# A new issue order on every engine, and a table of rooms for shared tiles, in a kernel of gated linear attention and top-2 expert attention

## The chip, the cores and the metric

One core of one Trainium2 chip runs the whole kernel in one launch. The metric is the device time of that launch in microseconds, as the median over runs; lower is better. The core's engines each run their own list of instructions in order: PE (TensorE, matrix products), DVE (VectorE), ACT (ScalarE, table functions and copies), POOL (GpSimd) and SP (SyncE, which here issues every DMA). They meet by semaphores.

## The reference

Two stages, for 4 batches, 8 heads, 768 time steps, head size 48; then 4 experts with heads of 64 over a model width of 384.

```python
# stage 1: gated linear attention with a complex decay, per head
a = (a_re, a_im) * min(|a|, 0.999) / (|a| + 1e-6)
for t in range(768):
    S = a[t] * S + k[t] v[t]^T          # complex state 48 x 48
    y[t] = q[t] . Re(S)
# stage 2: x = y with the heads side by side, [4, 768, 384]
w = softmax over the two largest of x @ w_gate
out = sum over experts e:  w_e * (causal softmax(q_e k_e^T / 8) v_e) @ wo_e
```

## The kernel before, in words

Stage 1 is done in chunks of 128 time steps. The running product of the decays becomes a sum of logarithms and a sum of angles, so that q and k can be turned by sines and cosines of the angle and scaled by exponentials; then a chunk is an ordinary masked product plus a term from the state of the chunk before.

`e_steps` makes this for one tile of 128 rows (three tiles, j = 0, 1, 2, per batch). Its steps, with the lines of the profile: squares and logarithms of the decay (L553, L558, and ACT's helper L360), inverses (L565, L569), the arctangent (L590), the angle in turns (L593), its running sum (L596), the wrap to one turn (L599 on POOL, L600 on DVE), the fold (L606), sine and cosine (L609, L610), the running sum of logarithms (L577), exponentials, and the products with q and k (L613, L616, L619, L625). Arctangent, sine and cosine need another function table than logarithm and exponential, so ACT visits that table: `visit` loads it (L370), runs the functions in it, and loads the first one back (L382). A load is an instruction of its own in ACT's list. Batch 0's three tiles share one visit at the start; the later tiles have one visit each, in which ACT also stands for them.

The results go through DMAs from SP into the layout of heads (`fm`, L664), and `p1_units` works on pairs of heads: transposes (`pk`, L686), scores of a chunk (`psc`, L693, masked on DVE into `pts`, L698), state updates (`pu`, L710, added on DVE into `wst1`, L720, copied by ACT to `tst`), and the output (`yu`, from `pts` at L731 and from the state `tst` at L738), which ACT copies to `x` and `yt`. `p2_units` is stage 2 on x: a split of x in two parts (`xth` on ACT, `xtl` on DVE, L777), values and gate (`pv`, L789), projections (`pp`, L838), a first pass for the row maxima (`pm`, L857 and L860), a regrouping by DMA (`stk`, L873 to L875), scores (`psS`, L908), the product with the values (`po`, L927), row sums (`dn`, L940), and the output projection (`pw`, L968).

Batch b's stage 2 lies beside batch b+1's stage 1. At the end of `attention_moe` every engine's instructions stand in a list in the order in which the program asked for them, and the table `ORDER` says in which order they are chained:

```python
for e, o in ORDER.items():
    for i, j in zip(o, o[1:]):
        tc.add_manual_dep(asked[e][j], asked[e][i].name, first_in, reason="order")
```

Two kinds of rooms matter. `ab` (decay and angles of a tile) and `qk` (q and k of a tile) have two rooms each, and batch 0's third tile lies in rooms that stage 2 uses later (`ab2`, `qk2`). PSUM's eight banks are two groups, three (`psa`: `pk`, `psc`, `pu`, `yu`) and five (`psu`: all else). A pool gives a new tile the next room by its own rule, and the tile waits until the room's last reader is done. `pace` and `hold` (L507 to L517) put idle products of a constant into PE's list, each waiting for a step of another engine.

Of the kernel before, what the change touches and what calls it, by code (L numbers as in the profile page):

```python
# [33 lines left out]
def pieces():  # L34

    out, f = [], 0
    while f < DM:
# [303 lines left out]
def attention_moe(ctx: ExitStack, tc: tile.TileContext, ak, vk, w, out):  # L341
# [882 lines left out]
    i, j = PL["lo"]  # L1224
# [72 lines left out]
```

## Time and profile before

| what | value |
|---|---|
| time, median of 3 runs | 543.96 us (542.48, 543.96, 556.38) |
| span of the profiled execution | 545.1 us |
| mean granted clock of TensorE | 0.921 |
| PE busy | 448.3 us (82% of the span) |
| ACT, DVE, POOL busy | 354.6, 349.4, 253.8 us |
| chain that ended last, by engine | PE 47%, DVE 17%, ACT 10%, DMA 10%, POOL 8%, issue 5% |

The span runs from the first instruction to the last. The profiled execution is a run of its own: its span is 1.14 us (0.2%) above the median of the runs. The granted clock is a share of 2.4 GHz; 0.5 is 1.2 GHz. The chain is followed back from the last instruction, at each step to what released it. In a timeline row the bracket says how long the engine stood idle ahead of the row and what ended that.

### The profile page before, as it was taken

Reading aid. Unit: us, or ns where it says so; the run is one execution under the profiler, and the core shown is the slowest. Engines: PE = TensorE matmul, PEld = TensorE weight load, DVE = VectorE, ACT = ScalarE, POOL = GpSimd, SP = SyncE. Lnnn points to the kernel's source line nnn. Section 1 sums busy time; section 2 is a strip of 40 time slices with the busy share of each in tenths; the row PEclk is TensorE's granted clock in tenths of the full one; section 3 lists DMA queues with packets and bytes.
Section 4 is the critical chain, followed back from the end, with each engine's and each line's share of the span. In section 5 each row is a group of like instructions: output and inputs, shape, how many; then the busy total and the mean of one; then the engine's idle time right before and its main releaser. Section 6 shows DMA issues by size and latency. Waiting matters only on the chain.

```text
span 545.1 us, 9176 instructions
## 1 busy us (share of the span) xinstructions
PE 448.3 (82%) x3376; PEld 348.7 (64%) x3376; DVE 349.4 (64%) x637; ACT 354.6 (65%) x751; POOL 253.8 (47%) x219
## 2 busy tenths in 40 slices
PE   0049996766895999986996998989599999989895
PEld 0016894665683775866784776669488876877564
DVE  6899845789548935667649472685883536456522
ACT  6827769948758557949469645887856547525363
POOL 5568614625255645825225482845423517202663
PEclk9988997789996998988695998999899999999989
DMA  8606492089331981499332675079542360456102
GB/s 334 273 0 174 118 298 74 13 194 220 98 88 30 259 191 37 125 226 212 111 84 58 203 162 152 8 169 242 133 117 59 80 133 16 134 127 140 35 2 87
DMA packets 23804, 71.10 MB, mean 130 GB/s; under 512 B 3312, under 2 KB 7632, under 8 KB 22736
## 3 DMA queue, kind: packets, MB, share of 16 engines
q1 hardware_dynamic: 23760, 70.53, 49.3%
q8 instruction: 26, 0.43, 0.3%
q14 instruction: 18, 0.15, 0.1%
HBM read 26.74 MB, written 4.72 MB: 58 GB/s over the span
## 4 chain that ended last, share of the span: by engine, by line
PE 47%; DVE 17%; ACT 10%; DMA 10%; POOL 8%; issue 5%; SPq 2%; ACTq 0%; POOLq 0%; DVEq 0%
PE po L927 6%; PE pp L838 6%; PE psc L693 5%; DMA stk<-qka 5%; POOL pe L931 4%; DMA ab<-in_ak_dram 4%; PE pm L857 3%; PE pw L968 3%; DVE ab L596 3%; PE psS L908 3%; PE pu L710 3%; ACT qk L360 3%; DVE qk L577 3%; PE psS L909 3%; PE dn L940 3%
## 5 line engine op out<-in xcount | busy, mean ns | idle before, releaser
L931 POOL TENSOR_TENSOR pe<-pe 128x512 f32<-128x512 f32 (+1 forms) x64 | 82.5, 1289 | 35.5 <-ACT r L360 15.8
L862 DVE TENSOR_REDUCE mx<-pm 128x1 f32<-128x384 f32 (+4 forms) x128 | 59.4, 499 | 25.1 <-PE pm L860 20.6
L360 ACT ACTIVATE pe<-psS 128x512 f32<-128x512 f32 (+2 forms) x96 | 47.1, 544 | 33.4 <-PE psS L909 30.7
L693 PE MATMUL psc<-fm 96*128 96x128 f32 x384 | 58.3, 292 | 8.4 <-ACT x L360 7.9
L915 POOL TENSOR_SCALAR_AFFINE_SELECT pe<-pe 128x256 f32<-128x256 f32 x48 | 24.6, 528 | 86.6 <-ACT pe L360 86.5
L360 ACT ACTIVATE qk<-qk 128x768 f32<-128x768 f32 (+5 forms) x105 | 56.3, 566 | 11.6 <-DVE qk L577 10.1
L693 PEld LDWEIGHTS psc<-fm 96*128 96x128 f32 x384 | 52.2, 204 | 10.4 <-ACT x L360 8.3
L908 PE MATMUL psS<-stk 128*128 128x256 f32 (+3 forms) x160 | 48.1, 335 | 3.9 <-DVE qka L845 1.4
L857 PE MATMUL pm<-qka,qz 128*128 128x384 f32 (+4 forms) x128 | 43.1, 404 | 5.1 <-POOL qk L581 3.1
L698 DVE TENSOR_TENSOR pts<-psc,keep 128x512 f32<-128x512 f32 x48 | 32.8, 684 | 20.3 <-PE psc L693 19.5
L509 PE MATMUL warm<-keep,identb 128*128 128x512 bf16 x44 | 15.7, 531 | 33.9 <-ACT ab L590 26.7
L909 PE MATMUL psS<-stk 65*128 65x256 f32 (+3 forms) x160 | 42.9, 309 | 0.8 <-DMA stk<-mr 0.8
L908 PEld LDWEIGHTS psS<-stk 128*128 128x128 f32 x160 | 31.3, 198 | 18.1 <-ACT xth L360 3.6
L738 PE MATMUL yu<-fm,tst 96*48 96x128 f32 x288 | 35.3, 288 | 8.3 <-ACT tst L360 8.3
L927 PE MATMUL po<-pe,v 128*64 128x256 f32 (+3 forms) x240 | 40.2, 423 | 0.3 <-POOL pe L915 0.3
L720 DVE TENSOR_TENSOR wst<-tst,pu 96x96 f32<-96x96 f32 x56 | 13.8, 246 | 38.8 <-ACT tst L360 17.2
L731 PE MATMUL yu<-pts,vt 128*64 128x128 f32 x360 | 38.5, 289 | 0.0
L360 ACT ACTIVATE tst<-wst,fm 96x48 f32<-96x48 f32 x112 | 31.0, 325 | 11.1 <-DVE wst L720 11.0
L710 PE MATMUL pu<-vt,kts 128*96 128x48 f32 x300 | 33.7, 248 | 3.1 <-DVE wst L720 3.1
L581 POOL TENSOR_TENSOR qk<-qk 128x768 f32<-128x768 f32 (+2 forms) x12 | 17.9, 1489 | 38.4 <-ACT qk L360 22.1
L710 PEld LDWEIGHTS pu<-vt,kts 128*96 128x96 f32 x300 | 30.7, 166 | 7.2 <-DVE wst L720 3.6
L565 POOL TENSOR_TENSOR ab<-ab 128x768 f32<-128x768 f32 x11 | 21.8, 1984 | 27.8 <-ACT ab L360 27.8
(143 smaller groups left out, 1184.2 us busy)
## 6 DMA issues: line engine op xcount, KB each, us to landing
fm<-qk SPq DMA_DIRECT2D x18, 578.2 KB, 6.0
ab<-in_ak_dram SPq DMA_DIRECT2D x12, 768.0 KB, 8.8
stk<-qka SPq DMA_DIRECT2D x16, 576.0 KB, 10.7
qk<-in_ak_dram SPq DMA_DIRECT2D x9, 768.0 KB, 5.7
stk<-qka SPq DMA_DIRECT2D x16, 384.0 KB
vt<-in_vk_dram SPq DMA_DIRECT2D x15, 384.0 KB, 7.2
fm<-qk SPq DMA_DIRECT2D x24, 192.8 KB, 3.7
out_dram<-ob SPq DMA_DIRECT2D x24, 192.0 KB, 1.9
```

Of the source, the lines that this page charges most:

```text
L360: ins = order["act"] = nc.scalar.activation(*a, **k)
L693: nc.tensor.matmul(p[:, cc, i, :], part(f, i, 1, c), part(f, i, 0, c), start=True, stop=True)
L698: nc.vector.tensor_mul(o, x, keep[:, None, :].to_broadcast([128, 4, C]))
L710: nc.tensor.matmul(pu[:, cc, i, :], kts[k][:, cc, i, :], v[c][:, i, :D], start=True, stop=True)
L731: nc.tensor.matmul(yu[64 * i:64 * i + 64, cc * C:(cc + 1) * C], v[2 * k + cc][:, i, :], pts[k][:, cc, i, :], start=True, stop=2 * k + cc == 0)
L738: nc.tensor.matmul(yu[64 * i:64 * i + D, cc * C:(cc + 1) * C], tst[c][:, i, :], part(f, i, 0, c), start=False, stop=True)
L857: nc.tensor.matmul(p[:, :s1 - s0], qz[:, e, tb * C:(tb + 1) * C], a[:, 3, s0:s1], start=True, stop=not last)
L862: nc.vector.reduce_max(m[:, col:col + 1], p[:, :s1 - s0], axis=AX.X)
L908: nc.tensor.matmul(y, s[:, 0, i * C:(i + 1) * C], s[:, 1, a0:t1], start=True, stop=False)
L909: nc.tensor.matmul(y, s[:65, 3, i * C:(i + 1) * C], s[:65, 2, a0:t1], start=False, stop=True)
L927: nc.tensor.matmul(po[64 * e:64 * e + 64, a0 - t0:t1 - t0], st.get("v2", v2)[:, i, pr, e], x[:, e], start=i == 0, stop=i == UNITS[g][-1][-1])
L931: on("sum").tensor_add(y, y, x)
```

## The change

Every list of `ORDER` is replaced. No instruction is added or removed, and each keeps its engine: PE 2480 matrix instructions, ACT 751, DVE 637, POOL 215 and SP 217 are the same set in both. Of PE's instructions 300 keep their place, and the others move by 12.9 places on average (67 at most); on ACT the mean is 4.9 (30), on DVE 4.2 (28), on SP 1.4, on POOL 1.0. Of 564 tiles in PSUM 305 follow another tile in their bank. The number of rooms of every tag stays. `pace(0)` no longer takes a tile.

```diff
 ORDER = {
-    'PE': (
-        0, 1, 2, 3, 4, 5, 6, 7, 8, 9, 10, 11, 12, 13, 14, 15, 16, 17, 18, 19, 20, 21, 22, 23, 24, 25, 26, 27, 28,
...
+    'PE': [
+        0, 1, 2, 3, 4, 5, 6, 7, 8, 9, 10, 11, 12, 13, 14, 15, 16, 17, 18, 19, 24, 25, 26, 27, 20, 21, 22, 23, 28, 29, 30, 31, 32, 36, 37, 38, 39, 40,
...
+SLOTS = {
+    'ab': [0, 1, 0, 1, 0, 1, 0, 1, 0, 1, 0, 1],
...
+    'psa': [0, 1, 2, 0, 1, 2, 0, 1, 2, 0, 1, 2, 0, 1, 2, 0, 2, 1, 2, 0, 1, 0, 1, 2, 0, 1, 2, 1, 0, 1, 2, 1, 1, 0, 2, 1, 0, 2, 2, 1, 1, 0, 2, 0, 0, 1, 2, 1, 0, 2,
...
+class Rooms:
+    def __init__(self, pool, bufs):
+        self.pool, self.bufs, self.made = pool, bufs, {}
+
+    def tile(self, shape, dtype, name, tag=None, bufs=None):
+        tag, bufs = tag or name, bufs or self.bufs
+        if tag in SLOTS:
+            i = self.made[tag] = self.made.get(tag, -1) + 1
+            tag, bufs = f"{tag}_{SLOTS[tag][i]}", 1
+        return self.pool.tile(shape, dtype, name=name, tag=tag, bufs=bufs)
...
-    sb = ctx.enter_context(tc.tile_pool(name="sb", bufs=2))
-    ps = ctx.enter_context(tc.tile_pool(name="ps", bufs=1, space=PS))
+    sb = Rooms(ctx.enter_context(tc.tile_pool(name="sb", bufs=2)), 2)
+    ps = Rooms(ctx.enter_context(tc.tile_pool(name="ps", bufs=1, space=PS)), 1)
...
     def pace(n):
-
+        if not n:
+            return
```

Line numbers of the changed kernel are lower by 7 up to `pace` and by 6 behind it, and its tile numbers by 3 or 4.

**First place: POOL in batch 0's start.** `ab_64`, `ab_66`, `ab2_68` are the angles of the three tiles, `qk_65`, `qk_67`, `qk2_69` their q and k. Before, POOL has:

```order
L593 TENSOR_SCALAR ab_66<-ab_66 128x768
L599 TENSOR_SCALAR ab_64<-ab_64 128x768
L599 TENSOR_SCALAR ab_66<-ab_66 128x768
L599 TENSOR_SCALAR ab2_68<-ab2_68 128x768
L616 TENSOR_TENSOR qk_65<-qk_65,ab_64 128x256 x2
L625 TENSOR_TENSOR qk_65<-qk_65,ab_64 128x256 x2
L616 TENSOR_TENSOR qk2_69<-qk2_69,ab2_68 128x256
L625 TENSOR_TENSOR qk_67<-qk_67,ab_66 128x256
```

With the change, where L593 is the wrap, L610 and L619 the products of k with sine and cosine, L575 and L581 the scaling of q and k:

```order
L593 TENSOR_SCALAR ab_64<-ab_64 128x768
L575 TENSOR_TENSOR qk_67<-qk_67 128x2x256
L593 TENSOR_SCALAR ab_66<-ab_66 128x768
L581 TENSOR_TENSOR qk2_69<-qk2_69 128x2x256
L619 TENSOR_TENSOR qk_67<-qk_67,ab_66 128x256
L610 TENSOR_TENSOR qk_65<-qk_65,ab_64 128x256
L593 TENSOR_SCALAR ab2_68<-ab2_68 128x768
L619 TENSOR_TENSOR qk_65<-qk_65,ab_64 128x256
L610 TENSOR_TENSOR qk_65<-qk_65,ab_64 128x256
L619 TENSOR_TENSOR qk_67<-qk_67,ab_66 128x256
L619 TENSOR_TENSOR qk_65<-qk_65,ab_64 128x256
```

The wrap of the third tile, `ab2_68`, moved from ahead of all products to behind two of them, which need sine and cosine of the first two tiles.

**Second place: SP at the end of batch 0's transfers.** `ab_516` and `qk_517` are the loads of batch 1's first tile (`ab_512` and `qk_513` with the change). Before:

```order
L664 DMA fm_258<-qk_65 64x1x514
L664 DMA fm_258<-qk_67 32x1x514
L664 DMA fm_258<-qk_67 96x1x514
L664 DMA fm2_266<-qk_67 96x1x514
L754 DMA x_322<-yt_411 16x3x256 x2
L664 DMA fm2_266<-qk_67 32x1x514
L664 DMA fm2_266<-qk2_69 64x1x514
L664 DMA fm3_509<-qk2_69 96x1x514 x2
L411 DMA ab_516<-in_ak_dram 128x1536
L416 DMA qk_517<-in_ak_dram 128x3x512
L411 DMA ab_520<-in_ak_dram 128x1536
```

With the change:

```order
L658 DMA fm_255<-qk_65 64x1x514
L658 DMA fm3_505<-qk2_69 96x1x514
L658 DMA fm2_263<-qk2_69 64x1x514
L404 DMA ab_512<-in_ak_dram 128x1536
L658 DMA fm3_505<-qk2_69 96x1x514
L409 DMA qk_513<-in_ak_dram 128x3x512
L404 DMA ab_516<-in_ak_dram 128x1536
L658 DMA fm2_263<-qk_67 96x1x514
L658 DMA fm2_263<-qk_67 32x1x514
L658 DMA fm_255<-qk_67 96x1x514
L658 DMA fm_255<-qk_67 32x1x514
L748 DMA x_319<-yt_408 16x3x256 x2
```

The load of batch 1's first tile moved ahead of five transfers to `fm` and of the pair to `x`, and that pair and four of the five now stand behind three loads.

**Third place: ACT at the last batch's first visit.** `kts_3712` and `tst_3687` (3708 and 3683 with the change) are copies for stage 1, `x_3671` (3667) the copy that empties the bank `yu_3664` (3660). Before, around the visit:

```order
L360 ACTIVATE ab_3404<-ab_3404 128x768 x2
L370 ACT_TABLE_LOAD
L609 ACTIVATE ab_2622<-ab_2622 128x768
L610 ACTIVATE ab_2622<-ab_2622,col_87 128x768
L590 ACTIVATE ab_3404<-ab_3404 128x768
L382 ACT_TABLE_LOAD
L360 ACTIVATE v2_103<-pv_3647 128x256
L360 ACTIVATE qk_3503<-qk_3503 128x3x256 x3
L360 ACTIVATE x_3671<-yu_3664 128x256
L360 ACTIVATE tst_3687<-wst1_3688,fm_3389 96x48 x2
L360 ACTIVATE v2_103<-pv_3697 128x256
L360 ACTIVATE kts_3712<-pk_3709 128x192
```

With the change:

```order
L353 ACTIVATE tst_3683<-wst1_3684,fm_3385 96x48 x2
L353 ACTIVATE kts_3708<-pk_3705 128x192
L353 ACTIVATE ab_3400<-ab_3400 128x768 x2
L363 ACT_TABLE_LOAD
L603 ACTIVATE ab_2618<-ab_2618 128x768
L353 ACTIVATE ob_3551<-pw_3544 128x384
L353 ACTIVATE ob_3625<-pw_3618 128x384
L353 ACTIVATE v2_103<-pv_3693 128x256
L604 ACTIVATE ab_2618<-ab_2618,col_87 128x768
L353 ACTIVATE tst_3688<-wst1_3689,fm_3385 96x48 x2
L353 ACTIVATE v2_103<-pv_3643 128x256
L353 ACTIVATE v2_103<-pv_3759 128x256
```

The copies `tst_3683` and `kts_3708` moved from behind the visit to ahead of it; `x_3667` stands four rows below the table load that ends the visit.

## Rows read from the trace of the kernel before

**Rows 1.** By stretch: length, engines' busy us, granted clock, DMA share, GB/s.
```profile
0.00:46.50 46.50, 12.63 (x32) 4.45 (x33) 39.63 (x56) 29.32 (x49) 28.62 (x28) 0.89 0.51 191
46.50:84.00 37.50, 37.39 (x397) 32.05 (x395) 25.62 (x52) 26.16 (x80) 19.10 (x16) 1.00 0.73 217
84.00:137.00 53.00, 35.31 (x206) 29.58 (x207) 41.80 (x61) 42.12 (x72) 25.38 (x18) 0.84 0.51 119
137.00:232.00 95.00, 84.28 (x663) 63.47 (x661) 58.65 (x107) 68.12 (x147) 50.55 (x42) 0.93 0.47 117
232.00:300.00 68.00, 55.38 (x376) 45.11 (x375) 47.91 (x91) 47.13 (x97) 24.84 (x17) 0.79 0.58 139
300.00:364.00 64.00, 60.43 (x468) 44.83 (x469) 37.03 (x62) 42.34 (x91) 36.28 (x32) 0.96 0.51 134
364.00:395.00 31.00, 23.88 (x181) 20.71 (x181) 23.05 (x42) 24.21 (x48) 14.53 (x9) 0.89 0.80 192
395.00:545.10 150.10, 138.97 (x1061) 108.49 (x1059) 75.70 (x171) 75.21 (x175) 54.48 (x59) 0.99 0.34 85
```

**Rows 2.** What TensorE waited for, whole run: total us, times, longest.
```profile
PE yu L738 <- ACT tst L360: 8.3, 5, 4.7
...
PE psc L693 <- ACT x L360: 7.9, 2, 4.9
```

**Rows 3.** POOL's timeline from 20 us: start, us, line, operation, tiles.
```profile
32.64 3.69 POOL L599 TENSOR_SCALAR ab<-ab 128x768 f32<-128x768 f32 x2 [1.69 <-DVE ab L596]
...
41.13 1.68 POOL L625 TENSOR_TENSOR qk<-qk,ab 128x256 f32<-128x256 f32 x2
...
59.08 6.05 POOL L625 TENSOR_TENSOR qk<-qk,ab 128x256 f32<-128x256 f32 x2 [0.86 <-DVE qk L616]
```

**Rows 4.** ACT's timeline from 36 us.
```profile
41.64 0.83 ACT L609 ACTIVATE ab<-ab 128x768 f32<-128x768 f32 x1
...
43.31 1.28 ACT L382 ACT_TABLE_LOAD   x1
```

**Rows 5.** DVE's timeline from 36 us.
```profile
35.56 2.44 DVE L600 SCALAR_TENSOR_TENSOR ab<-ab 128x768 f32<-128x768 f32 x2
...
39.38 1.29 DVE L613 TENSOR_TENSOR qk<-qk,ab 128x256 f32<-128x256 f32 x2
...
45.95 0.41 DVE L613 TENSOR_TENSOR qk<-qk,ab 128x256 f32<-128x256 f32 x1
...
60.27 1.75 DVE L501 TENSOR_TENSOR wlo<-wst,whi 128x1542 fp32r<-128x1542 f32 x1
```

**Rows 6.** PE's timeline from 46 us.
```profile
46.51 0.25 PE L686 MATMUL pk<-ident,fm 96*128 96x96 f32 x1
```

**Rows 7.** SP's queue from 36 us.
```profile
42.06 25.12 SPq L664 DMA_DIRECT2D fm<-qk  x26
...
71.32 0.59 SPq L411 DMA_DIRECT2D ab<-in_ak_dram  x1
```

**Rows 8.** The chain of waits, 60 to 137 us: start, us, what.
```profile
71.32 3.94 DMA ab<-in_ak_dram
...
77.12 1.47 POOL qk L553
```

**Rows 9.** ACT's timeline, 76 to 104 us.
```profile
82.67 1.28 ACT L370 ACT_TABLE_LOAD   x1
...
89.60 0.55 ACT L360 ACTIVATE tst<-wst,fm 96x48 f32<-96x48 f32 x2
```

**Rows 10.** ACT's timeline, 373 to 396 us.
```profile
376.81 1.28 ACT L370 ACT_TABLE_LOAD   x1
...
384.60 0.36 ACT L360 ACTIVATE x<-yu 128x256 f32<-128x256 f32 x1
```

**Rows 11.** PE's timeline, 382 to 396 us.
```profile
385.02 1.16 PE L693 MATMUL psc<-fm 96*128 96x128 f32 x8 [2.97 <-ACT x L360]
```

More of the change, by code (lines that the diff above doesn't have):

```diff
@@ L112 @@
 ORDER = {
[130 rows of a table removed]
-    ),
-    'Activation': (
[35 rows of a table removed]
-    ),
-    'DVE': (
[30 rows of a table removed]
-    ),
-    'Pool': (
[10 rows of a table removed]
-    ),
[11 rows of a table removed]
-    ),
-}
[101 rows of a table added]
+    'DVE': [
[22 rows of a table added]
+    'Activation': [
[27 rows of a table added]
+    'Pool': [
[15 rows of a table added]
+}
+SLOTS = {
[5 rows of a table added]
+    'psu': [0, 1, 2, 3, 4, 0, 1, 3, 4, 2, 0, 1, 3, 4, 2, 1, 0, 4, 3, 1, 3, 2, 0, 1, 0, 3, 4, 2, 1, 0, 3, 2, 4, 1, 3, 0, 2, 1, 3, 4, 2, 1, 4, 0, 2, 4, 3, 4, 1, 2,
[11 rows of a table added]
+    'psa': [0, 1, 2, 0, 1, 2, 0, 1, 2, 0, 1, 2, 0, 1, 2, 0, 2, 1, 2, 0, 1, 0, 1, 2, 0, 1, 2, 1, 0, 1, 2, 1, 1, 0, 2, 1, 0, 2, 2, 1, 1, 0, 2, 0, 0, 1, 2, 1, 0, 2,
[3 rows of a table added]
+    'kts': [0, 1, 0, 1, 0, 1, 0, 1, 0, 1, 0, 1, 0, 1, 0, 1, 0, 1, 0, 1, 0, 1, 0, 1, 0, 1, 0, 1, 0, 1, 0, 1, 0, 1, 0, 1, 0, 1, 0, 1, 0, 1, 0, 1, 0, 1, 0, 1, 0, 1],
+    'pts': [0, 1, 0, 1, 0, 1, 0, 1, 0, 1, 0, 1, 0, 1, 0, 1, 0, 1, 0, 1, 0, 1, 0, 1, 0, 1, 0, 1, 0, 1, 0, 1, 0, 1, 1, 0, 1, 0, 1, 0, 1, 0, 1, 0, 1, 0, 1, 0, 1, 0],
+    'tst': [0, 1, 2, 3, 4, 0, 1, 2, 3, 4, 0, 1, 2, 3, 4, 1, 0, 2, 3, 4, 1, 0, 2, 3, 4, 1, 0, 2, 3, 4, 1, 0, 2, 3, 4, 1, 0, 2, 3, 4, 1, 0, 2, 3, 4, 1, 0, 2, 3, 4,
[8 rows of a table added]
+}
+class Rooms:
[7 more added lines that the diff above has]
+        return self.pool.tile(shape, dtype, name=name, tag=tag, bufs=bufs)
 @with_exitstack
```

403 rows, old and new, of tables (ORDER, SLOTS) are left out of this document.

## The prediction

> **What bounds the kernel now.** I read the table by stretches first, then TensorE's list of waits, then the chain of waits and the engines' timelines at the places that the first two name. In the table [rows 1] a stretch's length less PE's busy time is PE's idle time. It is 33.9 us in 0 to 46.5, where stage 1 of batch 0 makes its first tiles; 0.1 up to 84; 17.7 in 84 to 137; 10.7 in 137 to 232; 12.6 in 232 to 300; 3.6 in 300 to 364; 7.1 in 364 to 395; and 11.1 behind that. So TensorE bounds most of the run, and an order can win only where it stands idle or at the lower clock. The granted clock is below 0.9 in three stretches behind the start: 0.84 in 84 to 137, 0.79 in 232 to 300 and 0.89 in 364 to 395 [rows 1]. The list of waits says what ends the idle time: output products that wait for a state copy of ACT, 8.3 us in five waits, 4.7 the longest, and chunk scores that wait for ACT's copy to x, which empties their bank, 7.9 us in two waits, 4.9 the longest [rows 2]. Both come from visits to the other function table. In the first, ACT loads the table at 82.67 and gets to the state copies at 89.60 [rows 9]. In the last batch it loads at 376.81 and gets to the copy to x at 384.60, and PE goes on at 385.02 after 2.97 us [rows 10, 11].
>
> **Part 1, batch 0's start: +4 us.** The wrap of the third tile now stands on POOL behind two products that need sine and cosine. Before, the second and third tile's wraps ended at 36.33 (32.64 + 3.69), ahead of all products, and the third sine began at 41.64 [rows 3, 4]. Now the DVE's list puts that tile's second wrap and fold behind ten products of the first two tiles. Ten products ran from 39.38 to 46.36 before, 7.0 us, some of them for the third tile (the first and the last stand in [rows 5]). The first sine comes some 1.3 us sooner, since a wrap and a fold no longer stand ahead of it; so the ten run from about 38.1 to 45.1. A wrap takes 1.22 (half of 2.44) and a fold 0.46 (a third of the time from 38.00 to the first product) [rows 5], so both end near 46.8 and the third sine is 5 us late. The table goes back 1.67 behind it, near 48.5 instead of 43.31 [rows 4]. On POOL the wrap, 1.85 us by half of the 3.69 for two, ahead of the cosine product and two products of 0.84 (half of 1.68) put the first product that the transfers wait for at an end near 45.6 instead of 42.0 [rows 3]. SP began its transfers at 42.06 [rows 7], PE its first pair at 46.51 [rows 6]; both move by 3.6, I take 4. Bounds: +2 if POOL's products run beside fewer DVE products than before, +6 if the third tile's 5 us come through whole. Nothing hides it: PE is busy 37.39 of the 37.5 us behind [rows 1], though idle products of a constant lie among them.
>
> **Part 2, batch 1's first tile: -9 us of waits, -2 of clock, +2 for ACT.** The load was issued at 71.32, landed after 3.94 us, and POOL began at 77.12, when the second load was there [rows 8]. It now passes seven transfers, at about 0.6 us of issue each (0.59 for the load itself, [rows 7]) 4.2 us; some 2 of the start's delay come back through products that it still stands behind. So it goes out near 68 to 69. More than that, its squares, logarithms and arctangent stand 25 places further ahead on ACT, between the copies of batch 0, and the first projections of batch 0's stage 2 stand on PE ahead of its last output products. The 4.7 us wait [rows 2] is covered by those. I estimate the tile's exponentials at 5 to 8 us sooner, and of the 17.7 us idle [rows 1] I take half, 9, as gone; bounds 3 (only the longest wait, less what follows late) and 14. The clock: 0.84 granted is 32% of the stretch at 1.2 GHz and the rest at 2.4 [rows 1]. Of the 35.31 us busy that is 11, which would take 5.6 less at the upper level. PE still waits at places, so I take 2; bounds 0 and 5.6. Against it stands ACT's own wait: a square of the new tile now lies in front of batch 0's state copies and waits for the load. If the load lands near 72 and ACT gets there near 70, PE's output products stand too. I take +2; bounds 0 and 5.
>
> At this place a row bears on the price. The two cosine products that POOL began at 59.08 took 6.05 us, against 1.68 for two at 41.13, and DVE's weight split of 1.75 us ran beside them [rows 3, 5]. In the new order the load stands behind the first of them, as the first of many transfers did before, so I add nothing.
>
> The Trainium skill, page "SBUF — State Buffer", section "Who interferes with whom", says that a DVE instruction with two inputs in SBUF contends with a GpSimd instruction that reads SBUF, and that the loser is fully blocked. The trace agrees: 6.05 against 1.68 us [rows 3]. By that rule, if both splits take the ports ahead of that product, the load would go out 3.5 us later (two splits of 1.75) and the forecast would be 535 us instead of 532.
>
> **Part 3, the later visits: -4 and -4 us.** In the last batch the state copies stand ahead of the visit, and the chunk scores take a bank emptied by such a copy, not by the copy to x. So the 2.97 us [rows 11] go, and with them part of the wait of the next state products, which stood behind them: 4 of the stretch's 7.1 us idle; bounds 0 and 6. At the visit whose wait is the 4.9 us the bank is changed in the same way, and the copy to x stands ahead: of the 4.9 us [rows 2] I take 3, and 1 for the clock, 0.79 there [rows 1]; bounds 0 and 7. What follows the copies there on ACT is the visit itself, which gets later by the copies (0.55 us for two, [rows 9]), so the sines of the next tile are late next; that is hidden by the tile's distance from its use.
>
> **Part 4, all else: -1 and +2 us.** In 137 to 232 the places move little: 1 of 10.7 us; bounds -4 and +2. In the stretches with little idle time (0.1, 3.6 and most of 11.1, [rows 1]) a new order finds nothing to win and can only lay waits: 305 new neighbours in PSUM, lists shaped to other durations. I take +2; bounds -4 and +6. Copies and products keep their durations, since nothing is added.
>
> **Sum.** +4 -9 -2 +2 -4 -4 -1 +2 = -12 us. The profiled span of 545.1 becomes 533.1. The span lies 1.14 above the median of the runs, so the forecast is 543.96 - 12 = 532.0 us.
>
> **The rivals.** (a) All gains come: ACT does not wait for the load, nothing new comes, and the waits in 137 to 300 shrink further. Then -9 -2 -4 -4 -1 is -20, and 4 more of the idle time in 137 to 300 pay for the start: 524 us. For it speaks that each named wait has its cause moved; against it, that the idle time behind each is a chain through ACT, DVE and POOL, and ACT is busy 42.12 of 53 us in 84 to 137 [rows 1].
>
> (b) The waits move instead of going: PE gets to the next thing that isn't there. Only the waits behind visits go (3 of 4.7, 3 of 4.9 and 2.97), less the start's 4 and 1 new: -4, 540 us. For it speaks DVE's and ACT's 41.80 and 42.12 us in 84 to 137 [rows 1], against it the 11 us in which they stand idle.
>
> (c) Slower: transfers to fm queued behind three loads. Four of the five now stand behind them. The first load took 3.94 us to land and the second 1.86 more (77.12 - 75.26) [rows 8]; three need 3.94 + 2 x 1.86 = 7.7 us. From 68 that is 76, and PE wants these tiles near 78. If the load goes out only at 72, as it does when the third tile's 5 us come through whole, the tiles land past 80, PE and ACT stand 4 us each in a stretch where PE was always busy, and the chain to 137 starts no sooner than before: +6 +4 +4, nothing of part 2, -6 of part 3: +8, 552 us. It decides from a load later than 71.32.
>
> (d) The order does not bind, because releases come in another order than the lists; then nothing moves, 544 us. Every list is chained whole, so I give this nothing of its own and count it with (b).
>
> **How the numbers follow.** The forecast has 0.44, (a) 0.20, (b) 0.22, (c) 0.14. 2% of the median, 10.9 us, is about what a measurement of this kernel can tell from no change: faster is below 533.1, slower above 554.8. Of the forecast's own range, 524 to 539, 0.27 lies on the faster side and 0.17 within; (a) is faster; (b) within; of (c) 0.06 is within and 0.08 beyond, by its bounds (+6 to +16). That makes 0.47 faster, 0.45 same, 0.08 slower. The range goes to 519, for (a) with the whole clock, and to 550, into (c).
>
> **What would show it.** Right: PE's first pair near 50, the table back near 48, the load of batch 1's first tile before 70, PE's idle time from 84 to 137 below 10 us, no wait over 2 us of chunk scores for a copy to x, and PE's idle time behind 395 unchanged. Wrong: a load after 71.3; PE waits for fm before 90; ACT standing over 4 us on the load; new waits above 3 us in 137 to 232 or 300 to 364; the clock in 84 to 137 not above 0.84.

## The result, and the profile after

The changed kernel takes 501.09 us (median of 4 runs, 495.03 to 504.97), against 545.91 for the kernel before beside it. The ratio is 0.912, with an interval of 0.904 to 0.920: 8.8% faster. That ratio compares the shorter runs of both kernels (of the changed one 497.82 and 495.03 us, at mean clocks of 0.966 and 0.976), while the profiled run is its longest, 504.97 us at 0.943, so the tables below are of a long run, and no profile shows where the shorter ones win 7 to 10 us more. The forecast was 532.0 us, and its range ended at 519, so the prediction was wrong: the sign is right, but the gain is over three times the size. The profiled execution has a span of 503.3 us, 41.8 less than before's 545.1.

The table by stretches of the changed kernel, cut where TensorE has done as many products as in [rows 1]; columns as there.

```profile
0.00:47.70 47.70, 12.42 (x32) 3.87 (x32) 40.16 (x58) 26.34 (x42) 29.11 (x28) 0.92 0.53 190
47.70:99.40 51.70, 50.02 (x397) 42.09 (x397) 34.01 (x61) 37.73 (x101) 21.63 (x21) 0.75 0.56 157
99.40:131.20 31.80, 28.29 (x209) 24.52 (x208) 25.76 (x47) 26.58 (x54) 15.70 (x11) 0.89 0.63 149
131.20:220.20 89.00, 82.37 (x666) 64.39 (x664) 68.12 (x110) 70.67 (x150) 52.92 (x45) 1.00 0.59 145
220.20:276.70 56.50, 50.38 (x378) 41.75 (x374) 44.00 (x88) 42.65 (x90) 23.75 (x17) 0.91 0.71 167
276.70:333.80 57.10, 55.89 (x470) 45.02 (x470) 39.29 (x65) 42.49 (x95) 36.66 (x33) 1.00 0.53 138
333.80:360.40 26.60, 22.62 (x185) 20.21 (x181) 19.66 (x47) 20.74 (x43) 9.72 (x6) 0.94 0.97 229
360.40:503.30 142.90, 135.15 (x1061) 109.21 (x1058) 77.86 (x170) 79.34 (x183) 58.50 (x62) 0.99 0.37 90
```

Row against row with [rows 1], in us of length: +1.2 in the start, +14.2 in the next stretch, -21.2, -6.0, -11.5, -6.9, -4.4 and -7.2; together -41.8. Up to 137 us of before that is -5.8, and behind it -36.0. Split another way: TensorE's idle time (length less its busy time) fell by 30.7 and its busy time by 11.1. Behind 137 the busy time fell by 16.5 for about as many products (2749 and 2760). The clock can account for the sum: one minus the clock, times the busy time of each row, is 24 us for the five rows of before and 7 for those of after. Over the whole run, where the products are the same, the same reckoning gives 35.4 and 24.9 us (0.921 of 448.3 us, 0.943 of 437.1), 10.5 of the 11.1. Row by row it fits less well (the last one lost 3.8 us of busy time at 0.99 in both, and what took them is open), since an equal number of products isn't the same products.

The waits of TensorE in the changed kernel, to set beside [rows 2]: total us, times, longest.

```profile
PE psc L687 <- ACT kts L353: 3.6, 1, 3.6
PE warm L503 <- ACT ab L603: 3.6, 1, 3.6
PE pk L680 <- DMA fm<-qk: 2.5, 4, 1.5
...
PE pk L511 <- DVE qk L613: 2.1, 4, 1.0
...
PE yu L732 <- ACT tst L353: 1.0, 3, 0.4
```

Both waits that the prediction was built on are gone: 8.3 us for state copies is 1.0, and 7.9 for the copies to x isn't in the list. Two stands of 3.6 us are new. One is in the start, for the third tile's late sine (the first row below); the other is at 346.20 in the last batch, where the scores now wait for another copy.

```profile
46.21 1.47 PE L503 MATMUL warm<-keep,identb 128*128 128x512 bf16 x4 [3.57 <-ACT ab L603]
```

A row that the prediction never read went with them: the idle products of `hold`, which wait for VectorE's product of q with the cosine, 2.1 us here. In the waits of before that row was:

```profile
PE pk L517 <- DVE qk L619: 8.4, 2, 5.2
```

### The profile page after: what moved, and what is told of

It reads as the page before. It is cut to its first block, busy times and chain, and to the rows that moved or that the text cites. A ratio compares the mean times of both kernels' runs of the same rounds, so it can differ in the third digit from the quotient of the medians.

```text
span 503.3 us, 9149 instructions
## 1 busy us (share of the span) xinstructions
PE 437.1 (87%) x3376; PEld 351.1 (70%) x3376; DVE 348.9 (69%) x637; ACT 346.5 (69%) x751; POOL 248.0 (49%) x219
## 5 line engine op out<-in xcount | busy, mean ns | idle before, releaser
L856 DVE TENSOR_REDUCE mx<-pm 128x1 f32<-128x384 f32 (+4 forms) x128 | 60.3, 499 | 12.5 <-PE pm L854 7.2
L687 PE MATMUL psc<-fm 96*128 96x128 f32 x384 | 63.6, 302 | 4.6 <-ACT kts L353 3.6
L909 POOL TENSOR_SCALAR_AFFINE_SELECT pe<-pe 128x256 f32<-128x256 f32 x48 | 22.9, 481 | 83.8 <-ACT pe L353 81.6
L687 PEld LDWEIGHTS psc<-fm 96*128 96x128 f32 x384 | 55.9, 210 | 9.0 <-ACT kts L353 4.5
L575 POOL TENSOR_TENSOR qk<-qk 128x768 f32<-128x768 f32 (+2 forms) x12 | 20.3, 1699 | 39.9 <-ACT qk L353 33.5
L704 PE MATMUL pu<-vt,kts 128*96 128x48 f32 x300 | 36.7, 257 | 0.6 <-DVE wst L714 0.6
L921 PE MATMUL po<-pe,v 128*64 128x256 f32 (+3 forms) x240 | 36.9, 396 | 0.0
L704 PEld LDWEIGHTS pu<-vt,kts 128*96 128x96 f32 x300 | 33.5, 176 | 4.8 <-issue 1.6
L503 PEld LDWEIGHTS <-identb 128*128 128x128 bf16 x44 | 5.3, 129 | 44.9 <-ACT ab L584 25.5
L353 ACT ACTIVATE kts<-pk 128x384 f32<-128x384 f32 (+1 forms) x48 | 20.4, 431 | 21.8 <-PE pk L680 15.4
L902 PEld LDWEIGHTS psS<-stk 128*128 128x128 f32 x160 | 29.6, 191 | 7.0 <-issue 3.4
```

The costliest lines, as they stand in the source:

```text
L353: ins = order["act"] = nc.scalar.activation(*a, **k)
L687: nc.tensor.matmul(p[:, cc, i, :], part(f, i, 1, c), part(f, i, 0, c), start=True, stop=True)
L704: nc.tensor.matmul(pu[:, cc, i, :], kts[k][:, cc, i, :], v[c][:, i, :D], start=True, stop=True)
L856: nc.vector.reduce_max(m[:, col:col + 1], p[:, :s1 - s0], axis=AX.X)
L902: nc.tensor.matmul(y, s[:, 0, i * C:(i + 1) * C], s[:, 1, a0:t1], start=True, stop=False)
L909: nc.gpsimd.affine_select(x[:, :, :C], x[:, :, :C], pattern=[[0, 2], [1, C]], base=0, channel_multiplier=-1, compare_op=OP.is_ge, fill=0.0)
```

## The experiments

All kernels compute the whole output. Most take the lists and rooms of one kernel up to a time in that kernel's profile, and those of the other behind. Their lines are shifted: L176 is ACT's copies, L334 `hold`, L436 the cosine product with q, L481 the transfers to fm, L510 `psc`, L548 and L555 `yu`, L186 and L198 the table loads.

### Where the gain lies: old and new order in halves

First the changed kernel again, with no edit, to see how far its runs differ.

> The changed kernel once more, on the same chip as the next three. Theory 1 (the granted clock of the stretch behind the start, 0.75 in the profiled run of 505 us, is what its slower runs lose): the time is 495 to 505 us; a profile of about 496 us shows PE busy some 8 us less than 437 with the difference between 48 and 99 us, and the same idle time, 66 us. Theory 2 (the slower runs lose by waits on other engines): PE idle time moves with the time, and the clock of that stretch does not.

Measured: 505.12 us (496.9 to 506.29, 4 runs), where before took 545.31 beside it. The profile is of a run of 504.75 us and shows a clock of 0.75 from 48.0 to 98.9 again; no run near 496 us was profiled, so the two theories can't be told apart. The runs of the changed kernel differ by some 2%, and a single profile of it isn't good to better than that.

```diff
 ORDER, SLOTS:
-    the changed lists and rooms
+    PE 32, ACT 48, DVE 56, POOL 24, SP 22 leading places of before (what begins before 46.4 us), the changed ones behind
```

> Order and rooms of before for all that began before 46.4 us (batch 0's start, up to PE's first pair), the new order and rooms behind it. Theory 1 (the third tile's late wrap costs at the start, PE stands 3.6 us on its sine, falls to 1.2 GHz and stays there): the stretch up to PE's 430th product, 99.4 us in the changed kernel's profile, ends 9 to 15 us sooner, and the whole takes 485 to 492 us. Theory 2 (the early part of the new order is a whole, and batch 1's early load needs its start): no gain or a loss, 496 to 508 us.

Measured: 501.81 us, ratio 0.9235 (0.918 to 0.929). The old start wins nothing. TensorE began as in before, but then stood 2.26 us for a transfer to fm, up to 55.15. The clock was 0.57 behind that, 0.50 from 60 to 68, and 1.00 again from 72.

```diff
+    PE 436, ACT 198, DVE 168, POOL 56, SP 72 leading places of before (up to 137 us), the changed ones behind
```

> Order and rooms of before for all that began before 137 us, the new ones behind. Theory 1 (each stretch keeps what the new order gains in it: 36 us lie behind 137 us by the two profiles, -5.8 us of offset there and -41.4 at the end): 506 to 514 us. Theory 2 (the later stretches gain because the front delivers sooner; the order behind 137 us is worth only the visits, 8 us and the clock): 525 to 538 us.

Measured: 508.52 us, ratio 0.936 (0.931 to 0.941). With the old order up to 137 us, and so with its 4.71 us wait for a state copy and its lower clock there, 36.8 us are won, where the changed kernel won 40.2 beside it (by the ratios 0.064, where the whole change has 0.088). So most of the gain lies behind 137, and is there without the new front. Its table behind that point, cut by the same counts:

```profile
136.60:162.00 25.40, 24.50 (x207) 19.07 (x207) 19.24 (x44) 20.67 (x49) 12.80 (x11) 1.00 0.31 88
162.00:221.80 59.80, 55.88 (x456) 44.07 (x458) 41.83 (x61) 45.60 (x98) 36.28 (x32) 1.00 0.59 154
221.80:276.30 54.50, 49.60 (x377) 41.56 (x372) 44.34 (x88) 42.58 (x90) 23.62 (x17) 0.91 0.72 172
276.30:334.30 58.00, 56.32 (x472) 45.17 (x470) 40.73 (x65) 42.76 (x95) 36.91 (x33) 1.00 0.53 136
334.30:362.40 28.10, 22.90 (x184) 20.53 (x181) 18.98 (x47) 20.80 (x43) 9.72 (x6) 0.88 0.90 217
362.40:505.30 142.90, 135.18 (x1061) 109.31 (x1058) 77.91 (x170) 79.46 (x183) 58.61 (x62) 1.00 0.37 90
```

Behind 220 each row is within 2.0 us of the changed kernel's, and the first two make 85.2, against 89.0 there and 95.0 in [rows 1].

```diff
+    PE 426, ACT 195, DVE 164, POOL 54, SP 69 leading places of the changed kernel (up to 131.2 us), before's behind
```

> The new order and rooms for all that began before 131.2 us in the changed kernel's profile, the old ones behind. Theory 1 (gains stay in their stretch): 5.8 us faster than before in a run like the profiled one and up to 14 in a run with the full clock behind the start, 530 to 540 us. Theory 2 (the front carries the gain through the run): 505 to 520 us.

Measured: 548.1 us (539.88 to 551.52), where before took 545.31: no gain that four runs with this spread can show. Its table shows where the front's 6 us went. It is at 130.80 where before is at 137.2, and has lost them by the end of the next row:

```profile
0.00:130.80 130.80, 88.87 (x634) 69.59 (x636) 99.75 (x164) 90.51 (x195) 66.42 (x58) 0.86 0.58 168
130.80:170.50 39.70, 29.22 (x211) 22.77 (x207) 25.77 (x51) 27.60 (x55) 18.41 (x16) 0.89 0.39 94
```

Rows of ACT and TensorE say where:

```profile
139.37 1.36 ACT L176 ACTIVATE qka<-pp 128x512 fp32r<-128x512 f32 x3 [3.64 <-DMA stk<-qka]
...
141.23 1.89 PE L334 MATMUL psS<-keep,identb 128*128 128x512 bf16 x4 [2.52 <-DVE mr L699]
...
170.49 0.50 PE L334 MATMUL pk<-keep,identb 128*128 128x384 bf16 x1 [5.21 <-DVE qk L436]
```

In before, the second of these stands here, with no wait ahead of it:

```profile
141.43 1.04 PE L517 MATMUL psS<-keep,identb 128*128 128x512 bf16 x4
```

So the lead is gone at 141. TensorE waits there for `mr`, a small step of VectorE (which is busy 10.22 of the 10.43 us up to then), and ACT's copy waits for the regrouping transfers. The last of these went out at 126.54, in before at 126.40, though TensorE was 6 us further, and it kept ACT until 139.37, in before until 135.53. By 149 x4 is 0.4 us behind before, and from 151 on 1.3 us, down to the product at 170.49, which in before began at 169.18 after 5.20 us. A front that brings TensorE forward doesn't bring these transfers forward with it.

### The clock in the start

```diff
- 'n3': (8, 8, 0, 0, 8, 2, 2, 4, 0),
+ 'n3': (8, 8, 0, 0, 8, 2, 14, 4, 0),
```

This adds twelve idle products behind the second tile's cosine, into the 3.57 us for which TensorE stood for the third tile's sine.

> The changed kernel with 12 more idle products in PE's list, behind the second tile's cosine, where PE then stood 3.6 us for the third tile's sine. Theory 1 (PE falls to 1.2 GHz because it stands there, and the stream of small products behind does not bring the clock back for 25 us): the clock between 48 and 72 us is near 1 instead of 0.50, PE's busy time in the stretch up to its 428th product falls from 49.4 by 8 to 12 us, and the whole takes 490 to 497 us in every run. Theory 2 (that stretch waits on the tiles of stage 1, and a faster PE only stands more): PE's idle time there grows by what its busy time loses, 500 to 506 us.

Measured: 504.15 us (494.04, 502.17, 506.14, 507.62), ratio 0.9253 (0.915 to 0.936). The profile is of the 494.04. First the changed kernel's clock from 46 us on (columns of [rows 1]; the clock is the third number from the end):

```profile
46.00:50.00 4.00, 3.66 (x13) 2.22 (x13) 3.37 (x6) 3.97 (x9) 3.08 (x5) 0.58 0.81 180
50.00:54.00 4.00, 3.92 (x22) 3.96 (x23) 2.97 (x6) 2.56 (x9) 2.85 (x3) 0.50 0.86 207
...
66.00:70.00 4.00, 4.00 (x28) 3.35 (x28) 3.88 (x5) 1.58 (x7) 1.88 (x1) 0.50 0.71 136
70.00:74.00 4.00, 4.00 (x19) 1.73 (x16) 0.25 (x1) 1.88 (x8) 0.70 (x2) 0.50 1.00 328
74.00:78.00 4.00, 4.00 (x36) 3.74 (x34) 0.51 (x3) 1.28 (x4) 1.89 (x2) 1.00 1.06 342
```

Then the filled one, whose first pair of transposes began at 47.65 us, as the changed kernel's did at 47.73:

```profile
43.50:47.50 4.00, 2.90 (x13) 0.97 (x11) 3.06 (x5) 2.14 (x3) 3.77 (x5) 1.00 0.65 142
47.50:51.50 4.00, 2.32 (x19) 1.97 (x19) 3.24 (x6) 3.99 (x12) 3.31 (x4) 1.00 0.86 206
51.50:55.50 4.00, 3.88 (x42) 3.58 (x43) 3.20 (x6) 2.23 (x9) 2.41 (x4) 1.00 0.83 229
```

From that pair to the first projection of x, the same work in both, the changed kernel (first row) and the filled one (second) need:

```profile
47.73:99.39 51.66, 50.00 (x396) 42.08 (x396) 33.97 (x61) 37.69 (x101) 21.59 (x21) 0.75 0.56 157
47.65:91.13 43.48, 39.48 (x397) 32.58 (x397) 32.44 (x61) 37.18 (x101) 25.30 (x21) 1.00 0.66 188
```

In the profiled run that is 8.2 us less, at full clock, with 4.0 us idle instead of 1.7. But the other three runs took over 502 us at mean clocks of 0.938 to 0.947 (the profiled one 0.970), and the changed kernel had runs of 495.03 and 497.82 us at 0.976 and 0.966 without the filling. So that the filling holds the clock isn't shown, and the median doesn't move.

### One engine's list alone

```diff
 ACT of before, at five visits (the third shown)
+    v2_103<-pv_2403
+    tst_2318<-wst1_2319,fm_2103 x2
     ACT_TABLE_LOAD (248.48)
...
     ACT_TABLE_LOAD (252.20)
-    tst_2318<-wst1_2319,fm_2103 x2
...
-    v2_103<-pv_2403
```

> The kernel before with 16 instructions moved in ACT's list alone, at five visits to the other function table: state copies and copies to x that were ready are put ahead of the visit or into it, and at two visits the new tile's square and logarithms are put ahead of copies that wait for PE. All other lists and all rooms are those of before. Theory 1 (most of what the new order gains behind 84 us is PE's waits behind visits, with the clock that falls after each): 515 to 525 us, PE's waits for ACT's x, for tst and for the products with cosine (8 us, 8 us, 8 us before) below 8 us together, the granted clock up from 0.92 to 0.94 or more. Theory 2 (the gain needs all lists, the visits are a small part): 533 to 542 us.

At the third visit the copy moved is that of `pv_2403`, and not the copy to `x_2377` for which TensorE waits there.

Measured: 550.36 us, ratio 1.006 (1.001 to 1.011): no gain from five edits. Nor did the waits go as meant: those for `tst` fell to 3.0 us, but those for the copies to x are 8.4 and those of `hold` 7.1. At the second place the square now stood ahead of its x copy, and ACT waited in it:

```profile
157.97 0.85 ACT L176 ACTIVATE qk<-ab 128x768 f32<-128x768 f32 x1 [4.19 <-DMA fm<-qk]
```

```diff
 ACT of before, one visit
+    v2_103<-pv_2403, tst_2318<-wst1_2319,fm_2103 x2
     ACT_TABLE_LOAD (248.48)
...
-    the same three, behind the visit
```

> The kernel before with three instructions moved in ACT's list: at the visit at 248 us the copy to x and two state copies stand ahead of the table load. Theory 1 (a wait costs itself and the clock behind it): PE's 4.9 us wait at 257 us goes, the clock from 256 to 268 us is 1 instead of 0.50, and the whole is 8 to 11 us faster. Theory 2, the prediction's own price (3 of the 4.9 us and 1 of clock, the next wait takes the rest): 3 to 5 us faster.

Here too the copy moved was that of `pv_2403`, which isn't ready until later. Measured: 547.6 us, ratio 1.002 (0.996 to 1.008). ACT stood 2.47 us for it with the visit behind, and TensorE's wait for the x copy grew from 4.90 to 5.65. So it says nothing on the question; the next run is the one that was meant.

```diff
 ACT of before, one visit
+    x_2377<-yu_2370, tst_2318<-wst1_2319,fm_2103 x2
     ACT_TABLE_LOAD (248.48)
...
-    the same three, behind the visit
```

> The kernel before with one move in ScalarE's list: the copy of x (x_2377 from yu_2370, at 256.71 in the profile of before) and the two tst_2318 copies stand ahead of the table load of 248.48 instead of behind the visit. The yu product is ready at 247.46, so the table load starts about 1.1 us later. Nothing else moves. Theory 1 (a wait removed is worth its length and the low clock behind it): the 4.9 us stand of TensorE before psc_2420 at 257 goes, the clock stays at full speed in 257 to 268, and the kernel is 5 to 9 us faster (ratio 0.983 to 0.991); in the profile psc_2420 starts near 252.5 to 253. Theory 2 (the engine meets its next wait, because the visit that it was waiting beside still ends when it did): psc_2420 starts near 253, but TensorE then stands 3 us or more within the next 15 us, and the time is within 3 us of before.

Measured: 546.6 us, where before took 546.55 beside it, ratio 1.0015 (0.997 to 1.006). The 4.90 us stand at 257 is gone, and the time is the same, as theory 2 says. TensorE's timeline shows what came in its place within 10 us, 4.33 and 3.16 us:

```profile
256.29 0.48 PE L548 MATMUL yu<-pts,vt 128*64 128x128 f32 x4 [4.33 <-ACT kts L176]
261.34 0.63 PE L674 MATMUL pm<-qka,qz 128*128 128x320 f32 x1 [3.16 <-DVE lg L610]
```

### One loop, several lists

The product at 169.18 ends a chain over five engines. In before SP sends two transfers to fm when TensorE has read the old fm room for the last time; they free a room of qk; ACT's square writes there; then POOL, the logarithms, the table load, sine and cosine, VectorE's product, and TensorE. SP's queue in before shows the first link:

```profile
151.16 0.35 SPq L421 DMA_DIRECT2D vt<-in_vk_dram  x1
151.62 19.60 SPq L664 DMA_DIRECT2D fm<-qk  x3
```

ACT's timeline in before shows the square, a copy that waits for TensorE, the logarithms and the load:

```profile
158.70 0.84 ACT L360 ACTIVATE qk<-ab 128x768 f32<-128x768 f32 x1
161.59 0.38 ACT L360 ACTIVATE x<-yu 128x256 f32<-128x256 f32 x1 [2.05 <-PE yu L738]
161.87 1.71 ACT L360 ACTIVATE ab<-ab 128x768 f32<-128x768 f32 x2
163.60 1.28 ACT L370 ACT_TABLE_LOAD   x1
```

And TensorE's row ends it:

```profile
169.18 0.50 PE L517 MATMUL pk<-keep,identb 128*128 128x384 bf16 x1 [5.20 <-DVE qk L619]
```

In the changed kernel the transfers go out at 143.33, and ACT does the rest with no copy to x in between:

```profile
151.23 0.85 ACT L353 ACTIVATE qk<-ab 128x768 f32<-128x768 f32 x1 [0.31 <-DMA fm<-qk]
...
155.17 1.28 ACT L363 ACT_TABLE_LOAD   x1
```

```profile
159.88 0.34 PE L511 MATMUL pk<-keep,identb 128*128 128x384 bf16 x1 [0.16 <-DVE qk L613]
```

The next run moves several links of this loop in before together.

```diff
 ACT of before
-    ab_975 (140.80), qk_996 x4 (142.29), ahead of tst_1140, tst_1193, x_1186
+    the five behind those and the copies after them
+    qk_1446<-ab_1015 (158.70), ahead of x_1186 (155.95)
+    ab_1015 x2 (161.87), ahead of x_1186 (161.59)
 POOL of before
-    qk_996, qk_996, pe_1329, pe_1362 x2, pe_1329 x2, ..., qk_1446
+    pe_1329, qk_996, pe_1362 x2, qk_996, pe_1329 x2, qk_1446, ...
```

> The kernel before with one loop's links moved together, on two engines, between 137 and 170 us. ScalarE: the five instructions of 140.80 to 144.35 (ab_975, qk_996) behind the tst and x copies that follow them; the square of ab_1015 (158.70) ahead of the x copy of 155.95; the two logs (161.87, 162.74) ahead of the x copy of 161.59. GpSimd: the two qk_996 products one and two places later, the qk_1446 product two places earlier. Theory 1 (the stand of 5.2 us before the hold product at 169.18 is the end of a loop over several lists, TensorE's last reads of the fm room, the fm transfers, the square, the logs, the table, VectorE's product, and it goes only if all links move): the fm transfers of 151.62 start 1.5 to 3 us earlier, the square near 154 to 155.5, the table load near 158 to 160, the hold product 3.5 to 6 us earlier (near 163 to 166) with a stand of 0 to 2.5 us before it, and the kernel is 3 to 6 us faster (0.989 to 0.995). Theory 2 (places move little here): the hold product stays within 1.5 us of 169.2 and the time within 2 us of before.

Measured: 542.09 us (12 runs) against 546.55, ratio 0.9939 (0.990 to 0.998), a gain of 3.3 us that the interval separates from none. The transfers went out at 148.54 and the square at 155.55, each 3.1 us sooner; but the loop gave most of it back, as ACT shows:

```profile
158.88 1.72 ACT L176 ACTIVATE ab<-ab 128x768 f32<-128x768 f32 x2 [1.08 <-POOL qk L370]
...
162.68 0.38 ACT L176 ACTIVATE x<-yu 128x256 f32<-128x256 f32 x1 [1.62 <-PE yu L555]
163.08 1.28 ACT L186 ACT_TABLE_LOAD   x1
```

The copy to x still stood ahead of the load, so the load came 0.5 us sooner and the product at 168.66, after 3.59 us instead of 5.20. That is theory 2's 168.66, not the 163 to 166 of theory 1, though the time is theory 1's. At equal numbers of products the two profiles stand at 200.1 and 200.1 us, and at 258.5 and 262.4: the profile puts the gain where nothing was edited, so what brings it is open. What the run does show is the chain: two links came 3.1 us sooner, and the first link that still waited for TensorE kept the end where it was.

```diff
 ACT
-    x_1186<-yu_1508 ahead of the table load
+    the same behind the visit's arctangent (L590)
 DVE
-    mx_1357<-pm_1504 ahead of qk_1446, qk_996 (L613, L619)
+    the same behind L619
```

> The kernel of x9_joint_move with the two links that were still old there: on ScalarE the copy of x that waited 1.62 us for TensorE at 162.68 stands behind the visit's cosine instead of ahead of its table load, and on VectorE the maximum that waited 3.72 us for TensorE at 163.58 stands behind the product q_cos (the write into qk at 166.31) instead of three instructions ahead of it. Theory 1 (the loop ends as late as its latest link, so the 3 us that the transfers and the square have won in x9 reach the hold product only now): table load at 160.5 to 161.5, q_cos from 163.5 to 164.7, the hold product at 165 to 166.5 with a stand of 0 to 1.5 us before it, and the kernel is 5 to 7.5 us faster than before (0.986 to 0.991). Theory 2 (x9's 3 us came from elsewhere, mostly the stands of 142 to 147): the hold product stays near 168 and the ratio near 0.994, or it comes earlier and TensorE meets a new stand of 2 us or more by 175.

Measured: 543.82 us against 548.25, ratio 0.9957 (0.991 to 1.000). The load came at 161.91, but the stand moved to scores that wait for the moved maximum:

```profile
168.91 0.55 PE L725 MATMUL psS<-stk 128*128 128x256 f32 x1 [3.82 <-DVE mx L679]
```

The sum of the stands is what it was, as in the second half of theory 2: each link taken out by hand laid the wait on another list.

### A better start

```diff
+    PE 112, ACT 86, DVE 83, POOL 35, SP 39 leading places of before (up to 60 us), the changed ones behind
```

> The order and rooms of before for all that begins before 60 us in its profile, the changed order behind. Theory 1 (the low clock and the waits of the changed kernel's start are the only thing wrong with it, and they come from its order up to 60 us): the products up to 84 us take 37 to 40 us at a clock above 0.95, the next stretch 31 to 35 as in the changed kernel, the rest as there: 486 to 493 us, ratio 0.89 to 0.905. Theory 2 (what the old start wins at first is lost again by 131, because the new order's work for the later stretches has not been done yet; as the front taken by itself was worth nothing): 497 to 504 us.

Measured: 495.38 us (493.18, 495.11, 495.65, 501.21), ratio 0.905 (0.899 to 0.911). It lies between the two theories. Beside the changed kernel's 0.912 (0.904 to 0.920) the intervals overlap, so that it beats it isn't settled. Its profile is of the 501.21, and there the stretch up to 97.8 takes 52.2 us at a clock of 0.81.

```diff
+    PE 256, ACT 127, DVE 107, POOL 39, SP 56 leading places of before (up to 84 us), the changed ones behind
```

> The order and rooms of before for all that begins before 84 us in its profile, the changed order behind. Theory 1 (the stretch up to 84 stays at 37.5 us, the next falls from 53 to 32 to 38 as its order is the new one): 486 to 496 us. Theory 2 (the next stretch's 53 us is set by what the start left undone, the load of the table at 71 and the work behind it, so it stays at 45 to 53): 500 to 510 us, as with the old order up to 137 (508.5).

Measured: 505.29 us, ratio 0.926 (0.920 to 0.932): theory 2. What the old order wins up to 84 us it loses by 131, at the seam between the two orders:

```profile
95.71 2.08 PE L655 MATMUL pp<-xth,whi 128*128 128x512 f32 x4 [12.10 <-ACT xth L176]
```

The new lists ask for the first projections here, and ACT makes `xth` only at 94.00, behind the work on batch 1's first tile, which the old front hadn't brought forward. So a cut of two orders also measures its seam.

Not tried: the changed lists with the old rooms, the new rooms with the old lists, and one engine's new list behind 137 with the others' old ones. So how much belongs to the lists and how much to the rooms is open.

## Why the prediction was wrong, point by point

**The front: right in sum by luck, with every part off.** Start, "batch 1's first tile" and the stretch between were forecast at +4 -9 -2 +2 = -5, and measure -5.8 in the profiled run. But the start cost 1.2, outside the bounds of +2 to +6: the third tile's sine came at 45.31 and the table went back at 47.00, nearly as late as reckoned, but SP's transfers began at 41.23, 0.8 us sooner than before and not 3.6 later. The stretch up to 84 grew by 14.2: its clock fell from 1.00 to 0.75 after the new 3.57 us stand. Its only term was a share of Part 4's +2. And 84 to 137 fell by 21.2, not 9; its idle time went from 17.7 to 3.5, and the load went out at 67.03, where 68 to 69 was forecast. These two stretches can't be read apart, since an equal count isn't the same products; together they give -7.0. The signs for this part came out: table back near 48, load before 70, idle below 10, clock above 0.84 (0.89), no wait over 2 us for copies to x. Only TensorE's first pair came at 47.73, not near 50. x4 shows that these 6 us are worth nothing with the old order behind them, and x3 that without them most of the gain stays.

**Part 4 is the step that failed: "the places move little" and "a new order finds nothing to win".** It gave -1 for 137 to 232 and +2 for three stretches with little idle time. The first measures -6.0, the three +14.2, -6.9 and -7.2; that they make +0.1 is two errors of 14 us that cancel. With the +2 laid on the two behind 300, Part 4 is short by 21 of the 30 us by which the sum was short: +1 against -20.1. x3 shows that such a gain comes with the old front too, so it belongs to the order and rooms behind 137. Of the 20.1 us, 9.8 are idle time (of 25.4) and 10.3 busy time. I read a busy TensorE as one at its best, and did not price the products that run at 1.2 GHz: one minus the clock, times the busy time, is 9.7 us in these three rows of before and 1.4 in those of after, so the clock can account for some 8 of the 10. The places do move: the 2180 matrix instructions that change theirs move by 14.7 on average, 69 at most (the 12.9 given with the change is the mean over all 2480). The sign "idle time behind 395 unchanged" was wrong as well (11.1 to 7.8).

**Part 3 was half its size.** -4 and -4 measure -11.5 and -4.4. The last batch is right in size, though not as told: the 2.97 us for the copy to x went and a 3.61 us stand of the scores for `kts` came. For 232 to 300 I took the named wait and 1 us of clock, and the stretch gave 6.5 of idle and 5.0 of busy time. The `hold` row there (3.22 us before) was never read.

**The reasoning on single waits was wrong in kind.** I priced each wait of TensorE by its own length. x8 takes one away, 4.9 us long, and nothing comes of it. x6 shortens the waits for `tst` and is no faster, though it left the other waits as long, so it says less. x4 brings TensorE 6 us forward, and within 11 us it waits these away for other engines. That favours rival (b) for any one edit. It does not hold for the whole change. My account is that there all links of a loop over lists and rooms moved at once. For the loop at 169 its links are seen in the rows of before, the changed kernel, x9 and x12, but neither x9 nor x12 opened it by hand, so that moving every link is enough is not shown. For the later stretches it is argued from the waits that went (2.1 us of `hold` in all, where 8.4 were), and no run here takes them one by one. x3 shows where the gain lies; which moves make it is open.

**The rivals.** (a) came nearest: the named waits went (8.3 to 1.0 us, and 7.9 to none in the list). It stopped at 524 since it took the gain for such waits alone. (c) did not come: the load was early, so the 3.5 us that the splits might have cost it did not come either, and waits for fm are 3.2 us in all, after 2.5. (Its 1.86 us for a second load were read from a row that names no releaser, only "issue".) (d) is out.

**The clock.** Of 41.8 us, 11.1 are busy time: +5.6 in 46 to 137 and -16.5 behind. I had 3. With the idle time of before at 96.8 us and of after at 66.2, the mean clock went from 0.921 to 0.943; that fewer stands raised it is argued from these numbers, and no run shows it by itself.

## What to carry to other kernels

Where every engine's list is fixed, don't price a wait by its length: ask what else must move for the work behind it to start sooner, and whether the change moves that too. An edit of one list gave 0 of 4.9 us here, and a new front 0 of 6; the new lists and rooms behind 137 us gave 36.8 us together. Read "busy" beside the granted clock in every stretch, since nearly half of the gain behind 137 us was busy time. And when forecasting a whole new order, let a stretch with little idle time win up to that idle time and what its lower clock costs: by [rows 1] 16.6 us in 137 to 232, 6.0 in 300 to 364 and 12.5 behind 395, where 6.0, 6.9 and 7.2 came.

## What the runs showed that I had not expected

After the 3.57 us stand in the start of the changed kernel the clock stayed at 0.50 from about 50 to 74 us, while TensorE was busy in 4.00 of 4.00 us in row after row. It was back at 1.00 behind eight idle products that began at 71.06. x1's profile shows the same: 0.50 from 48 to 72 us. With the stand filled (x5's profiled run) it was 1.00 all along, though TensorE had 4.0 us idle in that work instead of 1.7; as that is one run of four, it doesn't show that the filling did it. A long stand isn't needed for the fall either. In x10's profile TensorE's longest stand between 45.6 and 78 us is 1.24 us, and the clock fell at about 78:

```profile
76.00:80.00 4.00, 3.36 (x26) 2.94 (x28) 3.01 (x6) 3.99 (x12) 2.34 (x3) 0.75 0.22 38
80.00:84.00 4.00, 4.00 (x28) 3.58 (x26) 2.47 (x5) 3.07 (x7) 3.41 (x2) 0.50 0.49 181
```

It was 0.50 until about 102. So a profile's busy share doesn't tell the clock, and the list of waits doesn't tell where it falls: both are read beside the granted clock.
